# A list-scheduled transformer kernel: W2 loaded in two parts, task times corrected, and ranks for every step

## The chip, the cores and the metric

The kernel runs on one core of a Trainium2 chip. Time is device time in microseconds (us) of one execution, as the median of three runs; the profile is of one further execution of the same kernel. Engines are called by their names and by the short names of the profile: TensorE (PE, its weight loads PEld), VectorE (DVE), ScalarE (ACT), GpSimd (POOL) and SyncE (SP), whose queue issues the DMAs.

## The reference

Four layers over a sequence of 2048 rows of 512 in bfloat16: attention, MLP, attention, MLP, with the same weights both times. Attention is causal in a window of 256 rows, with 32 heads of 16.

```python
def _A_ref(x, wqkv, wo):
    B, S, D = x.shape
    H = 32; Dh = D // H; W = 256
    qkv = (x @ wqkv).reshape(B, S, 3, H, Dh).transpose(2, 0, 3, 1, 4)
    q, k, v = qkv[0], qkv[1], qkv[2]
    scores = jnp.einsum("bhqd,bhkd->bhqk", q, k) * (Dh ** -0.5)
    idx = jnp.arange(S)
    mask = (idx[:, None] - idx[None, :] >= 0) & (idx[:, None] - idx[None, :] < W)
    scores = jnp.where(mask[None, None], scores, -1e9)
    p = _softmax(scores, axis=-1)
    o = jnp.einsum("bhqk,bhkd->bhqd", p, v)
    return o.transpose(0, 2, 1, 3).reshape(B, S, D) @ wo

def _B_ref(x, w1, w2):          # w1: 512 x 1792, w2: 1792 x 512
    h = jnp.maximum(jnp.einsum("bsd,df->bsf", x, w1), 0)
    return jnp.einsum("bsf,fd->bsd", h, w2)

x = A_x
for layer in range(2):
    x = x + _A_ref(_layernorm(x), A_wqkv, A_wo)
    x = x + _B_ref(_layernorm(x), B_w1, B_w2)
```

## The kernel before

**Steps.** The sequence is cut into four chunks of 512 rows. A step is one chunk of one pair of layers (attention and MLP), so there are eight steps, k = 0 to 7; steps 4 to 7 are the second pair. In each step the chunk is normed and transposed (xnT), projected to Q, K and V (48 matmuls of 512 columns), attended, transposed again (OT), multiplied with wo, added to x, normed and transposed (xn2T), and sent through the MLP: 56 matmuls with W1 into hT and 56 with W2. Weights and x stay on the core.

**Attention.** K is spread into KBD and V into V2, ring buffers of 20 slots. Scores are made in groups into one PSUM tile of four banks (Sps); ScalarE takes the exponential of a group in one instruction of up to 2048 columns into Pb; GpSimd (with affine selects) or VectorE (with a minimum against the tile tri) sets masked entries to zero; TensorE multiplies with V2 into acc; VectorE divides. There are 156 score groups in all, 20 in a step and 16 in step 4. Their number along the sequence of groups is the "slot" in which most ranks of TensorE are counted.

**The planner.** The order of instructions is not written by hand. `plan_qkv`, `plan_attention` and `plan_rest` (lines 471, 541, 602) make tasks: `op(key, {engine: (us, function)}, deps, ...)` (line 229) with a rank `key`, the engines that can do the task with a time for each, and the tasks that it needs. Then a simulation of five engines walks through time. Whenever an engine is free, `choose` (line 734) takes one of its ready tasks: on TensorE that of lowest rank, on the others that of the lowest sum of ready time and rank. `begin` (line 755) emits its instructions at once. The result is one fixed order for each engine, and `InOrder` (line 104) chains each engine's instructions to keep it. On the chip, every engine works through its queue in that order and waits at semaphores; the planner's times play no part there any more.

A task with a third number, `(1.22, fn, 2.6)`, holds its engine for the first time and is complete after the second. SyncE's tasks have it: a transposing DMA of 128 rows (xnT, OT, xn2T) holds the queue for 1.22 us and lands 2.6 us after its start; the load of W2 (line 692) holds it for 1.4 us and lands after 9.0.

**Ranks on TensorE.** Scores have -100000 and their number, so they go first, in order. The multiplication with V2 has -50000 and more. wo has -10000 + k. Projections and MLP are filler with a rank in slots: those of a step `wait` = 16 slots ahead of its first score group (line 495), V at 1.6 slots from each other; those of the MLP spread from 7 to 24 slots after the end of the step's own scores (line 652), W1 over the first half and W2 over the second. Step 0 is worked in two halves (`HALVED`), with MLP parts from 8 to 18 slots after a given group (line 649). Dense matmuls share four PSUM buffers (`psum`, line 233).

**Other ranks.** `SOON` (line 194) has one rank for each kind of task, such as -1 for the copies to hT and for masks and -2 for additions to x. `calm` (line 477) holds back the norm statistics of steps 1, 2 and 3, by 1, 40 and 60. `act_free` (line 746) lets ScalarE take a task other than an exponential only if it ends at most 0.55 us after the next group can be exponentiated, or 0.1 us after a started group is done. If TensorE has had nothing for 0.4 us (line 802), the planner emits a filler matmul without use ("warm") against the slowing of the clock.

**Loads.** x and the weights come in at the start on SyncE's queue. W2 is a task of the planner: one DMA of 1.8 MB, free to go when the transposes of step 1's xnT (`applied[2]`) have landed.

Of the kernel before, what the change touches and what calls it, by code (L numbers as in the profile page):

```python
# [15 lines left out]
P = 128  # L16
# [22 lines left out]
]  # L39
PW = 576  # L40
SHOW = None

# [28 lines left out]
def kernel(  # L71
# [121 lines left out]

    SOON = {'qkv': -0.5, 'v': 0, 'h': -1, 'mask': -1, 'div': 0, 'add': -2}
    LINK = {"PE": 0.2, "DVE": 0.2, "ACT": 0.2, "POOL": 0.2, "SP": 0.2}

# [62 lines left out]

    EVAC = {512: {"DVE": 0.67, "ACT": 0.59}, 256: {"DVE": 0.42, "ACT": 0.38}}  # L260

# [20 lines left out]
    def norm_stats(lid, j, src, deps, eps_from=None, key=0):  # L282
        def fn():
            st = small.tile([P, 6], FP32, name="st", bufs=4)
            dve.bn_stats(out=st[:], in_=src)
            dve.bn_aggr(out=mvs[:, lid % 8, j, :], in_=st[:])
            if eps_from is not None:
                dve.tensor_scalar_add(rstds[:, lid % 8, eps_from:j + 1], mvs[:, lid % 8, eps_from:j + 1, 1], 1e-5)
        return op(key, {"DVE": (0.86 + (0.18 if eps_from is not None else 0), fn)}, deps)

    def norm_pow(lid, j0, j1, deps, key=0):
        r = rstds[:, lid % 8, j0:j1]
        return op(key, {"POOL": (0.72, lambda: pool.tensor_tensor(out=r, in0=r, in1=mhalf[:, j0:j1], op=ALU.pow))}, deps)

    def norm_apply(lid, j, src, deps, by_array, dst, then_key, dst_deps):

        box = Box(xns)
        mv, r, nb = mvs[:, lid % 8, j, :], rstds[:, lid % 8, j:j + 1], nbs[:, lid % 8, j:j + 1]

        def fn(e):  # L300
            box.t = box.tile([P, D], BF16, "xn")
            if e == "DVE":
                dve.tensor_scalar(out=box.t[:], in0=src, scalar1=mv[:, 0:1], scalar2=r, op0=ALU.subtract, op1=ALU.mult)
            else:
                pool.tensor_tensor(out=nb, in0=mv[:, 0:1], in1=r, op=ALU.mult)
                pool.tensor_scalar(out=nb, in0=nb, scalar1=-1.0, scalar2=None, op0=ALU.mult)
                pool.tensor_scalar(out=box.t[:], in0=src, scalar1=r, scalar2=nb, op0=ALU.mult, op1=ALU.add)
        times = {"DVE": 0.52} if by_array else {"POOL": 1.4, "DVE": 0.54}
        a = op(-10 if lid == 0 else 0, options(times, fn), list(deps) + list(dst_deps), box)
        if by_array:  # L310
            return transpose(then_key, lambda: box.t[:], lambda: dst[0][:, :, j * P:(j + 1) * P], [a], [box])

        def dma():
            sp.dma_start_transpose(out=dst[0][:, :, j * P:(j + 1) * P],
                                   in_=box.t[:].rearrange("p (kc d) -> p kc d", kc=KC))
        return op(0, {"SP": (1.22, dma, 2.6)}, [a], None, [box])

    def transpose(key, src, dst, deps, uses, take=None):
        box = Box(psum)

        def fn():
            box.ps = box.tile([P, KC, P], BF16, "tp")
            for kc in range(KC):
                pe.transpose(box.ps[:, kc, :], src()[:, kc * P:(kc + 1) * P], ident[:])
        t = op(key, {"PE": (0.26, fn)}, deps, box, list(uses) + [box])
        return op(0, options({"DVE": 0.42, "ACT": 0.59}, lambda e: copy(e, dst(), box.ps[:])), [t], take, [box])

# [119 lines left out]
    c_tri0 = op(-9, {"DVE": (0.2, lambda: dve.memset(tri[:], BIG))})  # L447
    c_tri = [op(3, {"POOL": (0.55, lambda i=i: triangle(i))}, [c_tri0]) for i in range(3)]
    c_v0 = [op(-6, {"POOL": (0.96, lambda s0=s0: pool.memset(V2f[:, 544 * s0:544 * (s0 + 4)].bitcast(FP32), 0.0))})
            for s0 in range(0, NSLOT, 4)]  # L450

    def v_ones(e):
        dve.memset(V2[64 * e:64 * e + 64, :, e, :, 16:17], 1.0)
    c_v = [op(-2, {"DVE": (0.4, lambda e=e: v_ones(e))}, c_v0) for e in range(2)]

# [15 lines left out]
    def plan_qkv(k):  # L471
# [4 lines left out]
        st, dst = [], []  # L476
        calm = (-10, 1, 40, 60)[k] if k < 4 else 0
        for j in range(4):
# [15 lines left out]
        old_pv = [pvs[n, j] for n in units_of.get(k - 2, []) for j in range(units[n].nq // 2)]  # L494
        wait = 0 if k == 0 else 16
        for h in range(2) if k == 0 else (None,):
# [5 lines left out]
            for t in range(4):  # L502
# [3 lines left out]
                def kmm(kc, ps, t=t, cols=cols):  # L506
                    mm(ps[:, cols], wqkv[:, kc, D + t * P:D + (t + 1) * P], xnT[0][:, kc, cols], kc == 0, kc == KC - 1)
                box, m = group(at, KC, us, kmm, need_x + [d_w[1]] + old[len(old) * t // 4:len(old) * (t + 1) // 4], lead=1000)
                times = {"DVE": 1.46, "ACT": 1.42} if h is None else {"DVE": 0.87, "ACT": 0.83}
                k_done[k, t, h or 0] = op(SOON["qkv"], options(times, lambda e, t=t, h0=h0, h1=h1, box=box:  # L510
                                                      spread_k(e, layer, c, t, h0, h1, box.ps)),
# [8 lines left out]
                def qev(e, t=t, cols=cols, box=box, idx=idx):  # L520
                    q = first(Q, (k, t), lambda: work.tile([P, 512], BF16, name="Qt", tag=f"Q{idx % 7}", bufs=1))
                    copy(e, q[:, cols], box.ps[:, cols])
                q_done[k, t, h or 0] = op(SOON["qkv"], options(EVAC[w], qev), [m2], None, [box])
                mine += [m, m2]
        for j in range(4):
            at = first_slot[units_of[k][0]] + (1 + (8 if j > 1 else 0) if k == 0 else 1.6 * j - wait)

            def vmm(kc, ps, j=j):
                mm(ps[:], xnT[0][:, kc, j * P:(j + 1) * P], wqkv[:, kc, 2 * D:3 * D], kc == 0, kc == KC - 1)
            box, m = group(at + 0.2, KC, 0.216, vmm, ([dst[j]] if k == 0 else dst) + [d_w[2]] + old_pv, lead=1000)  # L530
            vs = Box(stg)

            def vev(e, box=box, vs=vs):
                vs.t = vs.tile([P, 512], BF16, "Vst")
                copy(e, vs.t[:], box.ps[:])
            ev = op(SOON["qkv"], options(EVAC[512], vev), [m], vs, [box, vs])
            v_done[k, j] = op(SOON["v"], options({"POOL": 1.72, "DVE": 1.42} if k else {"POOL": 1.72, "DVE": 1.42, "ACT": 1.48}, lambda e, j=j, vs=vs: spread_v(e, layer, c, j, vs.t[:])),
                              [ev] + c_v, None, [vs])
            mine.append(m)

    def plan_attention(k):
        layer, c = divmod(k, NCH)
        prev = units_of.get(k - 1, []) if c else []
        for n in units_of[k]:
# [3 lines left out]
            for g in range(len(u.groups)):  # L548
# [17 lines left out]
                for m in u.masks(g):  # L566
                    times = {"DVE": 0.32 + 0.14 * (len(m) - 1), "POOL": 0.93 * len(m)}
                    masks[s].append(op(SOON["mask"], options(times, lambda e, m=m, g=g, pb=pb: mask(e, m, places(pb, g))), [exps[s]] + c_tri))
            for j0 in range(0, u.nq // 2, 2):
# [23 lines left out]
                def dfn(u=u, j=j, box=box):  # L593
# [3 lines left out]
                divs[k, u.t, j] = divs[k, u.t, j + 1] = op(  # L597
                    SOON["div"], {"DVE": (0.64, dfn)}, [prior] + war + checks[k - 2:k - 1], None, [box])
        checks.append(op(40, {"DVE": (1.1, lambda k=k: accumulate_check(chks[k % 2], k == 0))},
                         [divs[k, t, j] for t in range(4) for j in range(4)] + checks[-1:]))  # L600

    def plan_rest(k):
# [12 lines left out]
        for j in range(4):  # L615
# [8 lines left out]
            else:  # L624
                t = op(-5, {"SP": (1.22, lambda j=j, to=to: sp.dma_start_transpose(
                    out=to(), in_=O_of[k][:, j, :].rearrange("p (kc d) -> p kc d", kc=KC)), 2.6)}, ready, ob, [ob])
            turned[k, j] = t
# [4 lines left out]
            for o in [m]:  # L632
                o.uses.append(ob)
                ob.users += 1
            add = op(SOON["add"], {"DVE": (0.68, lambda j=j, box=box: residual(4 * c + j, box.ps[:], layer == 0))}, [m], None, [box])
            single = final and j >= 2
# [10 lines left out]
        for j0, j1 in ((0, 2), (2, 4)) if k in HALVED else ((0, 4),):  # L647
            if k in HALVED:
                d0 = first_slot[units_of[k][3 + 2 * j0]] + 8
                d1 = d0 + 10  # L650
            else:
                d0, d1 = base[k + 1] + 7, base[k + 1] + 24
            n0, n1 = P * j0, P * j1
            evs = []
            for f in range(NF):
# [6 lines left out]
                def hev(e, f=f, box=box, n0=n0, n1=n1):  # L662
                    if hT[0] is None:
                        hT[0] = work.tile([P, NF, 512], BF16, name="hT", tag="hT", bufs=1)
                    copy(e, hT[0][:, f, n0:n1], box.ps[:, n0:n1], True)
                evs.append(op(SOON["h"], options(EVAC[n1 - n0], hev), [m], None, [box]))
            for j in range(j0, j1):
                for n0, n1 in ((0, 256), (256, 512)) if final and j == 3 else ((0, 512),):
# [14 lines left out]
                    else:  # L683
                        x_done[k, j] = op(SOON["add"], {"DVE": (0.68, lambda j=j, box=box: residual(4 * c + j, box.ps[:], False))},
                                          [m, x_done[k, j], dst[j]], None, [box])

    plan_qkv(0)
    for k in range(NSTEP):
        plan_attention(k)
        if k == 0:  # L690
            plan_qkv(1)
            d_w2 = op(0, {"SP": (1.4, lambda: sp.dma_start(w2[:], B_w2.rearrange("(f p) n -> p f n", p=P)), 9.0)}, applied[2])
        plan_rest(k)
# [52 lines left out]
    def act_free(t, us):  # L746
# [4 lines left out]
        if scores[s].number in started:  # L751
            return t + us <= score_end[0] + 0.1
        return t + us <= max(t, scores[s].at("PE")) + 0.55

# [21 lines left out]
    while events and events[0][0] < 3000:  # L776
# [16 lines left out]
        for e in ENGINES:  # L793
# [7 lines left out]
            elif e == "PE" and done_ops[0] < len(ops) - 12:  # L801
                if t - idle_since[0] >= (0.4 if t > 20 else 0.0) and sum(1 for f, _ in psum.free if f <= t) > 1:
                    box = Box(psum)
# [166 lines left out]
```

## Time and profile before

| what | value |
|---|---|
| time, median of 3 | 482.74 us (481.2 to 483.36) |
| span of the profiled execution | 481.4 us |
| instructions | 14229 |
| exponentials on ScalarE | 282.6 us, 156 instructions |
| masks on GpSimd | 218.9 us, 498 instructions |
| transposing DMAs | 28 each of xnT, OT and xn2T, 2.5 us to landing |
| W1 and W2 | one DMA of 1792 KB each |

The page lists each engine's busy time and its share of the span, then the chain that ended last, followed backwards from the last instruction to what released it. Stage tables give, for a stretch of time, its length, the busy time of an engine with the number of its instructions, the clock that was granted to TensorE (1.00 is full), the share of time in which the DMA engines moved data, and GB/s. A timeline line has start, duration, engine, source line, operation, output and input, shape and count; in brackets stands the idle time before it and what ended it. Almost every instruction is recorded under line 114, the helper that all engines' calls go through, so one goes by the names of the tiles: ps_d is the output of a dense matmul, "w" stands for W1 and W2, Sps for scores, acc for the product with V.

### The profile page before, as it was taken

The page shows a single profiled execution, that of the slowest core. Times are in us where ns is not written, and L with a number is a line of the kernel's source. Part 1 is how long each engine was busy: PE and PEld are TensorE (multiplying, and loading weights), DVE is VectorE, ACT ScalarE, POOL GpSimd, SP SyncE. Part 2 cuts the span into 40 slices and gives each one's busy share as a digit, 9 for nine tenths or more (in the row PEclk, how much of TensorE's full clock was granted, in tenths as well). Part 3 has the DMA queues.
Part 4 walks back from the last instruction along what each step waited for, and adds up shares of the span by engine and source line. Part 5 has one row for each costly group of instructions (what it writes and reads, how often), then busy time and mean ns, then how long its engine had stood idle before and what let it go on. Part 6 is the DMA issues. An engine that isn't in the chain of part 4 may idle for free.

```text
span 481.4 us, 14229 instructions
## 1 busy us (share of the span) xinstructions
PE 457.3 (95%) x5893; PEld 244.7 (51%) x5967; DVE 354.4 (74%) x852; ACT 336.6 (70%) x263; POOL 299.5 (62%) x665
## 2 busy tenths in 40 slices
PE   8899999998999989999999999999999999999995
PEld 3555646654555534555554555544555545464443
DVE  6989988867986688977998878797558875464101
ACT  3878777876878657887778777777768777644230
POOL 7788878656786786856885766685766647421000
PEclk9999999999999989999999999999999999999998
DMA  8870321004300052002221023010331103000101
GB/s 247 276 200 3 67 23 25 2 3 67 59 9 3 8 84 45 3 3 45 57 35 33 15 23 67 11 38 2 45 78 25 34 1 68 25 1 11 34 12 38
DMA packets 54791, 21.96 MB, mean 46 GB/s; under 512 B 46144, under 2 KB 54208, under 8 KB 54720
## 3 DMA queue, kind: packets, MB, share of 16 engines
q1 hardware_dynamic: 54720, 20.98, 20.3%
q8 instruction: 48, 0.79, 0.7%
q14 instruction: 23, 0.19, 0.2%
HBM read 7.86 MB, written 2.10 MB: 21 GB/s over the span
## 4 chain that ended last, share of the span: by engine, by line
PE 77%; DVE 7%; POOL 5%; DMA 5%; issue 3%; ACT 1%; POOLq 0%; SPq 0%; DVEq 0%; ACTq 0%
PE ps_d L114 54%; PE acc L114 14%; PE Sps L114 8%; DMA OT<-O 3%; POOL Pb L114 3%; DVE KBD L114 2%; DVE st L114 1%; ACT Pb L114 1%; DVE x_sb L114 1%; POOL xn L114 1%; DMA xnT<-xn 1%; DVE Pb L114 1%; POOL rstds L114 1%; DMA x_sb<-in_A_x_dram 1%; DVE xn L114 1%
## 5 line engine op out<-in xcount | busy, mean ns | idle before, releaser
L114 ACT ACTIVATE Pb<-Sps 128x2048 bf16<-128x2048 f32 (+2 forms) x156 | 282.6, 1811 | 92.6 <-PE Sps L114 75.6
L114 POOL TENSOR_SCALAR_AFFINE_SELECT Pb<-Pb 64x256 bf16<-64x256 bf16 x498 | 218.9, 440 | 111.8 <-ACT Pb L114 91.6
L114 PE MATMUL ps_d<-xn2T,w 128*128 128x512 bf16 (+1 forms) x481 | 105.3, 355 | 2.5 <-issue 1.0
L114 PE MATMUL ps_d<-w,hT 128*128 128x512 bf16 (+1 forms) x438 | 103.8, 376 | 2.1 <-issue 1.3
L114 PEld LDWEIGHTS <-Pb 128*128 128x128 bf16 x2880 | 84.2, 96 | 26.6 <-issue 9.3
L114 PE MATMUL acc<-V2f,Pb 128*128 128x34 bf16 x2880 | 90.6, 178 | 2.6 <-POOL Pb L114 1.5
L114 DVE TENSOR_TENSOR Pb<-Pb,tri 128x512 bf16<-128x512 bf16 (+1 forms) x141 | 60.3, 433 | 16.5 <-ACT Pb L114 15.6
L114 PEld LDWEIGHTS <-w 128*128 128x128 bf16 x504 | 45.4, 97 | 44.6 <-issue 6.1
L114 PE MATMUL ps_d<-xnT,wqkv 128*128 128x512 bf16 (+1 forms) x277 | 64.9, 355 | 2.0 <-ACT KBD L114 0.9
L114 PEld LDWEIGHTS <-hT 128*128 128x128 bf16 x462 | 42.4, 98 | 46.6 <-issue 6.0
L114 PE MATMUL Sps<-Qt,KBD 32*128 32x320 bf16 (+3 forms) x1488 | 60.8, 251 | 1.3 <-ACT Pb L114 0.9
L114 DVE TENSOR_SCALAR hT<-ps_d 128x512 bf16<-128x512 f32 (+1 forms) x79 | 48.1, 619 | 16.3 <-PE ps_d L114 16.0
L114 PEld LDWEIGHTS <-KBD 32*128 32x128 bf16 x1488 | 23.4, 92 | 46.1 <-issue 42.9
L114 DVE TENSOR_SCALAR KBD<-ps_d,par 128x256 bf16<-128x256 f32 (+1 forms) x80 | 44.2, 601 | 1.4 <-PE ps_d L114 1.3
L114 DVE BATCH_NORM_STATS2 st<-x_sb 128x6 f32<-128x512 f32 (+1 forms) x64 | 43.7, 682 | 1.2 <-DMA x_sb<-in_A_x_dram 0.7
L114 DVE TENSOR_TENSOR x_sb<-ps_d,x_sb 128x512 f32<-128x512 f32 x48 | 32.4, 682 | 12.1 <-PE ps_d L114 11.4
L114 ACT ACTIVATE hT<-ps_d 128x512 bf16<-128x512 f32 (+1 forms) x47 | 26.2, 559 | 21.1 <-PE ps_d L114 21.1
L114 PEld LDWEIGHTS <-wqkv 128*128 128x128 bf16 x288 | 26.1, 97 | 25.6 <-issue 3.2
L114 PE MATMUL ps_d<-wo,OT 128*128 128x512 bf16 x121 | 32.6, 384 | 5.2 <-DMA OT<-O 4.4
L114 DVE TENSOR_TENSOR ob<-ps_d,x_sb 128x512 bf16<-128x512 f32 (+1 forms) x17 | 11.2, 659 | 34.4 <-PE ps_d L114 33.3
L114 POOL TENSOR_TENSOR rstds<-rstds,mhalf 128x2 f32<-128x2 f32 (+1 forms) x33 | 24.3, 738 | 16.7 <-DVE rstds L114 14.6
L114 PE MATMUL ps_d<-wqkv,xnT 128*128 128x512 bf16 x119 | 31.6, 379 | 0.3
(55 smaller groups left out, 279.9 us busy)
## 6 DMA issues: line engine op xcount, KB each, us to landing
w<-in_B_w_dram SPq DMA_DIRECT2D x2, 1792.0 KB, 10.6
out_dram<-ob SPq DMA_DIRECT2D x15, 128.0 KB, 1.7
wqkv<-in_A_wqkv_dram SPq DMA_DIRECT2D x3, 512.0 KB, 7.0
x_sb<-in_A_x_dram SPq DMA_DIRECT2D x3, 512.0 KB, 9.0
x_sb<-in_A_x_dram SPq DMA_DIRECT2D x2, 256.0 KB, 3.0
wo<-in_A_wo_dram SPq DMA_DIRECT2D x1, 512.0 KB, 8.8
xnT<-xn SPq DMA_TRANSPOSE x28, 2.5
OT<-O SPq DMA_TRANSPOSE x28, 2.5
```

Source lines behind the costliest of these rows:

```text
L114: inst = fn(*a, **k)
```

## The change

The planner stays, and so do all tasks of the computation. Three things change.

1. W2 is loaded by two DMAs of half the size, each planned as holding SyncE's queue for 3.6 us and landing after 5.0, the second after the first, with rank 3 in place of 0. In the plan no transposing DMA is issued during these 3.6 us. The aim is to keep the load and the transposes apart.
2. Times of tasks are corrected to those of a trace: VectorE's eviction of 512 columns 0.67 to 0.69, norm statistics 0.86 to 0.91, the power on GpSimd 0.72 to 0.75, the norm's application on GpSimd 1.4 to 1.58 and on VectorE 0.54 to 0.6, spreading V 1.72 to 1.85 on GpSimd and 1.42 to 1.35 on VectorE, masks, the division 0.64 to 0.72, the addition 0.68 to 0.69, and the landing of a transposing DMA 2.6 to 2.9.
3. Ranks that were one number for a kind of task are looked up in a table by kind and step, `tune(name, k, value)`, where `value` is the old number. The table has 98 entries: the ranks of SOON per step, of the norm's application, of the norm statistics ("calm"), the lead of the projections ("wait") and the pace of V, the start and length of the MLP ("from", "span"), ScalarE's allowance ("slack") and the idle time before a filler matmul ("idle", 0.4 to 0.81). The aim is an order with less waiting.

Two helpers that are added, `norm_stats_act` and `eps_op`, are called by nothing.

```diff
+TUNE = {
+    ("ones", 0): 3.74,
+    ("tri", 0): 2.04,
+    ("turn", 0): -0.63,
+    ("apply", 0): -14.88, ("apply", 1): -3.07, ("apply", 2): -3.19, ("apply", 3): -3.23, ("apply", 4): -1.45,
...
+    ("idle", 0): 0.81,
+    ("slack", 0): 0.91, ("slack", 1): 0.32,
+    ("qkv", 0): -3, ("qkv", 1): 0.71, ("qkv", 2): -0.94, ("qkv", 3): 0.47, ("qkv", 4): -2.62, ("qkv", 5): 1,
...
+    ("calm", 0): -6.45, ("calm", 1): 49.78, ("calm", 2): 55.35, ("calm", 3): 50.68,
+    ("wait", 1): 18.52, ("wait", 2): 20.9, ("wait", 3): 19.33, ("wait", 4): 15.48, ("wait", 5): 8, ("wait", 6): 9.3,
+    ("wait", 7): 18.77,
+    ("pace", 1): 0.2, ("pace", 2): 1.32, ("pace", 3): 1.71, ("pace", 4): 0.37, ("pace", 5): 1.05, ("pace", 6): 1.21,
+    ("pace", 7): 2.79,
+    ("from", 1): 6.7, ("from", 2): 5.71, ("from", 3): 4.61, ("from", 4): 11.02, ("from", 5): 9.1, ("from", 6): 3.64,
+    ("from", 7): 5.18, ("from", (0, 0)): 12.67, ("from", (0, 2)): 15.26,
+    ("span", 1): 29.93, ("span", 2): 16.39, ("span", 3): 33.16, ("span", 4): 36, ("span", 5): 16.73,
+    ("span", 6): 18.08, ("span", 7): 28.64, ("span", (0, 0)): 10.73, ("span", (0, 2)): 6.75,
+}
+def tune(name, k, value):
+    return TUNE.get((name, k), value)
...
+    def soon(name, k):
+        return tune(name, k, SOON[name])
...
-        return op(0, {"SP": (1.22, dma, 2.6)}, [a], None, [box])
+        return op(0, {"SP": (1.22, dma, 2.9)}, [a], None, [box])
...
-        calm = (-10, 1, 40, 60)[k] if k < 4 else 0
+        calm = tune("calm", k, (-10, 1, 40, 60)[k] if k < 4 else 0)
...
-        wait = 0 if k == 0 else 16
+        wait = 0 if k == 0 else tune("wait", k, 16)
...
-                d0 = first_slot[units_of[k][3 + 2 * j0]] + 8
-                d1 = d0 + 10
+                d0 = first_slot[units_of[k][3 + 2 * j0]] + tune("from", (k, j0), 8)
+                d1 = d0 + tune("span", (k, j0), 10)
             else:
-                d0, d1 = base[k + 1] + 7, base[k + 1] + 24
+                d0 = base[k + 1] + tune("from", k, 7)
+                d1 = d0 + tune("span", k, 17)
...
-            d_w2 = op(0, {"SP": (1.4, lambda: sp.dma_start(w2[:], B_w2.rearrange("(f p) n -> p f n", p=P)), 9.0)}, applied[2])
+            w2_in, d_w2 = B_w2.rearrange("(f p) n -> p f n", p=P), None
+            for f0, f1 in ((0, NF // 2), (NF // 2, NF)):
+                d_w2 = op(3, {"SP": (3.6, lambda f0=f0, f1=f1: sp.dma_start(w2[:, f0:f1, :], w2_in[:, f0:f1, :]), 5.0)},
+                          applied[2] + [d_w2])
...
-            return t + us <= score_end[0] + 0.1
-        return t + us <= max(t, scores[s].at("PE")) + 0.55
+            return t + us <= score_end[0] + tune("slack", 1, 0.1)
+        return t + us <= max(t, scores[s].at("PE")) + tune("slack", 0, 0.55)
...
-                if t - idle_since[0] >= (0.4 if t > 20 else 0.0) and sum(1 for f, _ in psum.free if f <= t) > 1:
+                if t - idle_since[0] >= (tune("idle", 0, 0.4) if t > 20 else 0.0) and sum(1 for f, _ in psum.free if f <= t) > 1:
```

## The prediction

> **What bounds the kernel now.** I read the page first: busy time by engine, then the chain that ended last.
>
> ```profile
> PE 457.3 (95%) x5893; PEld 244.7 (51%) x5967; DVE 354.4 (74%) x852; ACT 336.6 (70%) x263; POOL 299.5 (62%) x665
> ...
> PE 77%; DVE 7%; POOL 5%; DMA 5%; issue 3%; ACT 1%; POOLq 0%; SPq 0%; DVEq 0%; ACTq 0%
> ```
>
> TensorE is busy for 95% of the span and carries 77% of the chain; no other engine is above 74%. The change neither adds nor removes a matmul of the computation. So what it can win lies in two places only: TensorE's idle time, 481.4 - 457.3 = 24.1 us, and the filler matmuls ("warm") that the planner puts where it finds nothing ready. Next I cut the span into stages for TensorE (stage, busy time and count, granted clock, DMA share, GB/s):
>
> ```profile
> 10.00:30.00 20.00, 17.48 (x236) 1.00 0.80 251
> 30.00:50.00 20.00, 19.62 (x280) 1.00 0.28 78
> 50.00:70.00 20.00, 17.90 (x258) 1.00 0.33 50
> ...
> 100.00:122.00 22.00, 19.09 (x244) 1.00 0.30 46
> 122.00:170.00 48.00, 47.26 (x692) 1.00 0.10 19
> 170.00:182.00 12.00, 10.19 (x92) 0.86 0.44 69
> ...
> 280.00:420.00 140.00, 137.65 (x1851) 1.00 0.20 35
> ```
>
> The reader is to see that the holes are in the first 182 us. Idle time is 2.5, 2.1, 2.9 and 1.8 us in the stages 10-30, 50-70, 100-122 and 170-182; from 280 to 420 us it is 1.7% and made of pieces under 0.2 us where TensorE changes from one kind of work to another. The first 10 us (2.1 idle) are the first loads, the last 5.4 us are the last addition and store: neither is touched. The same stages for the filler give 2.1 us in 40-60, 3.4 us in 100-122, none after 140, and 7.4 us in the first 10. Then the timeline of TensorE in two holes:
>
> ```profile
> 113.00 0.81 PE L114 MATMUL warm<-ident 128*128 128x512 bf16 x3
> 114.02 0.40 PE L114 MATMUL Sps<-Qt,KBD 32*128 32x192 bf16 x8 [0.21 <-ACT Pb L114]
> 114.35 0.82 PE L114 MATMUL warm<-ident 128*128 128x512 bf16 x3
> ...
> 118.27 1.90 PE L114 MATMUL ps_d<-wo,OT 128*128 128x512 bf16 x8 [1.43 <-DMA OT<-O]
> ...
> 176.08 0.60 PE L114 MATMUL ps_d<-wo,OT 128*128 128x512 bf16 x2 [1.50 <-DMA OT<-O]
> ```
>
> These are two kinds of hole. Around 110-121 the planner itself saw nothing to do and filled: the projections of step 2 and the MLP of step 0 were used up, and the MLP of step 1 was not yet possible. At 116.8 and 174.6 the plan believed that OT would be there and it was not. The DMA issues say why: three or more transposes follow each other at 1.3 us, and then the later ones take longer. The first line is SyncE's timeline there, the second is over all 28 of OT.
>
> ```profile
> 112.75 4.95 SPq L114 DMA_TRANSPOSE OT<-O  x3
> ...
> DMA to landing us min/median/max: 2.4/2.5/4.2
> ```
>
> **What the Trainium skill says.** "TensorE: Matmul & The Clock Gate", part 2 (What happens when you issue a matmul): matmuls stay in program order, only weight loads are pulled ahead. The trace agrees: at 174.6 everything waited 1.50 us for one OT. So an order that is wrong at one place stops the whole engine. The same page, part 1: an idle window halves the clock. The row 170-182 shows 0.86, (1 - 0.86) x 12 = 1.7 us lost, after idle time of only 1.50 us; the equal hole at 116.8 cost no clock, so I count this half. "Perfetto Trace Analysis", Identifying the Most-Contended Engine, warns that matmul busy time overstates; the trace agrees (379 ns for a 512-column matmul that follows its neighbour after 0.22), so idle plus filler is a lower bound on the waste. "DMA: Bandwidth & Descriptors", Issuing engines are not separate DMA queues: all transfers share 16 engines and interleave. That bears on W2, next.
>
> **The change, part by part.**
>
> *W2 in two parts.* W2 is issued at 26.24 and takes
>
> ```profile
> DMA to landing us min/median/max: 8.1/8.1/8.1
> ```
>
> so it lands at 34.3; its first reader runs at 62.0. Two OT transposes are issued beside it at 32.77 and 34.02 and land 2.4 to 2.5 us later, the normal time, and in 30-40 TensorE is busy for 9.89 of 10 us: the sharing cost nothing visible. Half of W2 is 4.1 us (8.1/2) at best and, with the fixed part from the 256 KB load that took 3.0 us, 3.0 + 0.66 MB x (5.1 us / 1.57 MB) = 5.1 us at worst. Both parts end by 26.2 + 10.2, or some 10 us later if they give way to transposes; the 28 us of slack hide either. One more issue is 0.6 us of SyncE, which is idle. Behind it in SyncE's queue stand the OT transposes; in the plan each part holds that queue for 3.6 us. If both held up a transposition that TensorE needed, that would cost up to 7.2 us, against 0 if none. I take 0: at this place the transposes come 6.5 us after the last xnT issue.
>
> *Task times.* These only steer the plan. The new ones are nearer to the rows: the residual 0.69 (682 ns), hT on VectorE 0.69 (688 ns), statistics 0.91 (685 + 182 ns and a gap), division 0.72 (252 + 424 ns and a gap). Each correction is 0.01 to 0.18 us. The one that touches the holes is the transposition, 2.6 to 2.9; but the traces' late ones took 3.9 to 4.2. Of an error of 1.5 us, 0.3 is mended. So the waits for OT are not planned away; they go only where other work happens to stand in front.
>
> *Ranks.* These decide which ready task each engine takes. For TensorE the ones that count are the places of the projections ("wait" 16 becomes 8 to 21 score slots of lead) and of the MLP ("from", "span": 17 slots become 16 to 36). MLP(0) goes from 8 slots to 13 and 15: it is held back, and dense work is left for the hole at 110-121. A slot is 415/156 = 2.7 us, so 7 slots are 19 us. The wider spans (33 and 36 for steps 3 and 4) leave more for the pure dense tail after 428 us, which runs at 55.16 busy of 56, so nothing is lost there. For VectorE, "calm" of step 1 goes from 1 to 49.78, so its norm statistics run only when VectorE has nothing else; four times 0.87 us (685 + 182 ns), needed before the projections of step 1 at 29 us, are at risk. Steps 2 and 3 stood at 40 and 60 already. For ScalarE, "slack" rises from 0.55 to 0.91: an eviction may hold up an exponential by 0.36 us more. TensorE waits for exponentials for 0.9 us in all, so this is hidden while dense work is at hand.
>
> *The sum*, hole by hole. The share is my choice, by whether the planner can see the hole.
> - 10-30: 2.5 idle. The chain there is GpSimd (masks, V2, rstds); ranks reorder it but don't shorten it. A third: 0.8.
> - 40-70: 2.1 filler + 2.1 idle, of which 0.9 is a wait for OT. Half: 2.1.
> - 100-122: 3.4 filler + 2.9 idle, of which 2.0 is for OT. Mostly visible to the plan: 60% of 6.3 is 3.8.
> - 170-182: 1.8 idle + 1.7 clock, unplanned. Half: 1.7.
> - The other stages: 0, switching.
>
> Together 8.4. A new order in one in-order queue brings waits of its own kind; today's unplanned ones are worth 4.4 (all of TensorE's waits for OT), and I charge a quarter of these, 1.1. Net 7.3 to 7.4: 482.74 - 7.4 = 475.3.
>
> **The rivals.**
> *A, as above*, 475.3, in a band of 470 to 480.
> *B, all holes go*: 2.5 + 4.2 + 6.3 + 3.5 = 16.5 us, so 466.3. For it: there is dense work without end later (428 to 475 is nothing else), and 98 values are enough to place it. Against it: GpSimd binds in 10-30, and OT lateness isn't in the plan.
> *C, no change*: holes at 110-121 are filled, but transposes that come in threes and fours make as many new waits; 8.4 back and forth, 482. For it: the wait for OT is the longest named wait of TensorE (4.4 us, 4 times). Against it: filler is 5.4 us that the planner saw.
> *D, slower*: an order fitted to the plan to hundredths of a us breaks on the chip at another place, and one more hole like 100-122 (6.3) arises while only 2 are won: 482.7 + 6.3 - 2 = 487. For it: late statistics of step 1 ("calm" 49.8) and an MLP held too long (span 36 where a step has 20 slots, with one hT buffer, so that the next MLP waits for its last matmul). Against it: the planner knows these waits, and its TensorE costs (0.216 per matmul) are those of the trace.
>
> **How the numbers follow.** A 0.53, B 0.17, C 0.14, D 0.16. The range of 468 to 484 leaves out half of B and most of D, about 0.2. Within 0.5% means 480.3 to 485.2. Faster: A, B and a little of C, 0.73. Same: most of C with the edge of A, 0.11. Slower: D, 0.16.
>
> **What would show it.** If right: TensorE's busy time hardly falls except for the filler, its idle time falls from 24 to about 18; in the stage table the rows up to 122 us gain most; filler after 40 us shrinks from 20 matmuls to under 10; W2 shows two issues with no wait of TensorE near them, and its first reader doesn't wait for DMA. Waits for OT remain, 2 to 5 us. The last exponential may move, the dense tail gets longer or shorter by the same amount. Wrong: filler or idle time as before in 100-122 (C), a wait for statistics or xnT in 25-35 or for W2 near 62, a second stage with a clock under 1 (D), or a stage table without holes (B).

## The result, and the profile after

| what | before | after |
|---|---|---|
| time, median | 481.97 us (480.87 to 483.36) | 476.81 us (475.97 to 479.01) |
| ratio, 95% interval | | 0.9899 [0.9853, 0.9944] |
| span of the profiled execution | 481.4 us | 474.6 us |

The change makes the kernel faster by 5.2 us, 0.6 to 1.5%; 475.3 was predicted, within 468 to 484. (The forecast was a gain of 7.4 us, counted from the 482.74 that was then the median; the median of before in the table is 0.8 lower, so the time was met more closely than the gain.) The two profiled executions differ by 6.8 us, since the one of before (483.17 us) was above its median; its granted clock was 0.993, and most of before's executions have 0.996 or more. In what follows, one trace shows where time lies, and the medians how much it is.

The page of the changed kernel, busy time, chain and W2's issues (size of each, us to landing):

```profile
PE 451.7 (95%) x5890; PEld 242.8 (51%) x5963; DVE 348.1 (73%) x845; ACT 345.9 (73%) x277; POOL 299.4 (63%) x664
...
PE 82%; ACT 5%; DVE 5%; DMA 3%; issue 3%; POOL 2%; SPq 0%; ACTq 0%; DVEq 0%; POOLq 0%
...
w<-in_B_w_dram SPq DMA_DIRECT2D x2, 896.0 KB, 6.4
```

The share of TensorE in the chain rose from 77 to 82%: there is less of others to wait for. Its idle time is 474.6 - 451.7 = 22.9 us, hardly less than 24.1. Busy time fell by 5.6 us, though no matmul of the computation is gone. The filler is 1.8 us of that, and 1.7 us, as an estimate from the clock, is the stretch of half clock in before (177.6 to 181.0 us), in which matmuls take longer. The other 2.1 us aren't resolved; the recorded ends of matmuls may overlap differently when kinds of work alternate in another order. So idle time alone is not the measure here; the holes have to be counted by stage, with filler and clock. The stages of TensorE after (stage, busy time and count, clock, DMA share, GB/s):

```profile
10.00:30.00 20.00, 17.44 (x241) 1.00 0.58 192
30.00:50.00 20.00, 16.67 (x248) 1.00 0.60 133
50.00:70.00 20.00, 19.40 (x269) 1.00 0.14 28
...
100.00:122.00 22.00, 20.71 (x279) 1.00 0.30 50
122.00:170.00 48.00, 46.59 (x683) 1.00 0.18 32
170.00:182.00 12.00, 11.78 (x178) 1.00 0.15 30
```

The same stages for the filler matmuls alone:

```profile
10.00:30.00 20.00, 1.55 (x7) 1.00 0.58 192
30.00:50.00 20.00, 2.53 (x10) 1.00 0.60 133
...
100.00:122.00 22.00, 0.00 (x0) 1.00 0.30 50
```

and in before:

```profile
10.00:30.00 20.00, 0.27 (x1) 1.00 0.80 251
30.00:50.00 20.00, 2.05 (x8) 1.00 0.28 78
...
100.00:122.00 22.00, 3.36 (x12) 1.00 0.30 46
```

The reader adds, for each stage, idle time (length less busy time), filler, and what a clock under 1 takes:

| stage | before | after | change | predicted |
|---|---|---|---|---|
| 10-30 | 2.5 + 0.3 filler | 2.6 + 1.6 filler | +1.3 | -0.8 |
| 30-70 | 2.5 + 2.1 filler | 3.9 + 2.5 filler | +1.9 | -2.1 (for 40-70) |
| 100-122 | 2.9 + 3.4 filler | 1.3 | -5.0 | -3.8 |
| 122-170 | 0.7 | 1.4 | +0.7 | 0 |
| 170-182 | 1.8 + 1.7 clock | 0.2 | -3.3 | -1.7 |
| all others | | | -0.3 | 0 |
| new waits, no place named | | | | +1.1 |

They sum to -4.7 us of the 6.8 between the two spans; the other 2.1 are the unresolved busy time. The late holes went nearly whole; the early ones grew. The waits of TensorE (us in total, times, longest) name what is left, first in before, then in the changed kernel:

```profile
PE ps_d L114 <- DMA OT<-O: 4.4, 4, 1.5
...
PE Sps L114 <- ACT Pb L114: 0.9, 3, 0.5
...
PE tp L114 <- DVE xn L114: 0.5, 1, 0.5
```

```profile
PE Sps L150 <- ACT Pb L150: 3.0, 10, 0.6
PE tp L150 <- DVE xn L150: 2.2, 2, 2.0
...
PE ps_d L150 <- DMA OT<-O: 1.2, 2, 0.9
PE ps_d L150 <- DMA xnT<-xn: 1.2, 1, 1.2
```

Waits for OT fell from 4.4 to 1.2 us; waits for the exponential and for the first norm (xn, at 11.45 us) rose from 0.9 to 3.0 and from 0.5 to 2.2. The timeline of TensorE shows the place of step 1's projections and of wo in step 1:

```profile
40.94 0.81 PE L150 MATMUL ps_d<-xnT,wqkv 128*128 128x512 bf16 x3 [1.23 <-DMA xnT<-xn]
...
117.01 1.90 PE L150 MATMUL ps_d<-wo,OT 128*128 128x512 bf16 x8 [0.85 <-DMA OT<-O]
```

The projections of step 1 now begin at 40.9 us, since its statistics come late ("calm" 49.78). W2 follows them on SyncE's queue (start, time on the queue):

```profile
35.95 3.62 SPq L150 DMA_TRANSPOSE xnT<-xn  x2
39.62 1.18 SPq L150 DMA_DIRECT2D w<-in_B_w_dram  x2
```

The parts of W2 land at 45.0 and 47.6 us; TensorE first reads hT and W2 at 68.0. No wait of TensorE names W2.

### The profile page after: what moved, and what is told of

Read it like the earlier page. It is cut to its first block, busy times and chain, and to the rows that moved or that the text cites. A ratio compares the mean times of both kernels' runs of the same rounds, so it can differ in the third digit from the quotient of the medians.

```text
span 474.6 us, 14227 instructions
## 1 busy us (share of the span) xinstructions
PE 451.7 (95%) x5890; PEld 242.8 (51%) x5963; DVE 348.1 (73%) x845; ACT 345.9 (73%) x277; POOL 299.4 (63%) x664
## 4 chain that ended last, share of the span: by engine, by line
PE 82%; ACT 5%; DVE 5%; DMA 3%; issue 3%; POOL 2%; SPq 0%; ACTq 0%; DVEq 0%; POOLq 0%
PE ps_d L150 59%; PE acc L150 13%; PE Sps L150 9%; ACT Pb L150 4%; DMA OT<-O 2%; DVE V2f L150 1%; POOL Pb L150 1%; DMA xnT<-xn 1%; DMA x_sb<-in_A_x_dram 1%; PE tp L150 1%; DVE st L150 1%; DVE Pb L150 0%; DVE Vst L150 0%; POOL rstds L150 0%; DVE xn L150 0%
## 5 line engine op out<-in xcount | busy, mean ns | idle before, releaser
L150 POOL TENSOR_SCALAR_AFFINE_SELECT Pb<-Pb 64x256 bf16<-64x256 bf16 x504 | 221.8, 440 | 98.5 <-ACT Pb L150 72.2
L150 PEld LDWEIGHTS <-Pb 128*128 128x128 bf16 x2880 | 82.9, 96 | 21.3 <-issue 9.4
L150 PE MATMUL acc<-V2f,Pb 128*128 128x34 bf16 x2880 | 88.3, 178 | 0.7 <-POOL Pb L150 0.3
L150 DVE TENSOR_TENSOR Pb<-Pb,tri 128x256 bf16<-128x256 bf16 (+1 forms) x143 | 59.9, 429 | 16.9 <-ACT Pb L150 15.6
L150 PE MATMUL ps_d<-xnT,wqkv 128*128 128x512 bf16 (+1 forms) x275 | 63.3, 355 | 2.3 <-DMA xnT<-xn 1.2
L150 DVE TENSOR_SCALAR hT<-ps_d 128x512 bf16<-128x512 f32 (+1 forms) x66 | 39.6, 607 | 16.4 <-PE ps_d L150 15.7
L150 ACT ACTIVATE hT<-ps_d 128x512 bf16<-128x512 f32 (+1 forms) x60 | 33.9, 568 | 23.5 <-PE ps_d L150 22.2
L150 DVE TENSOR_SCALAR xn<-x_sb,mvs,rstds 128x512 bf16<-128x512 f32 (+1 forms) x45 | 25.0, 575 | 13.2 <-issue 9.3
L150 PE MATMUL ps_d<-wo,OT 128*128 128x512 bf16 x118 | 31.3, 380 | 1.9 <-DMA OT<-O 1.2
```

Of the source, the lines that this page charges most:

```text
L150: inst = fn(*a, **k)
```

## The experiments

Each comparison had its own runs of the kernel before, with medians of 481.97 to 482.3 us. The theory behind the first six: the gain is one of ranks, TensorE's above all, since W2 and the times bring no work forward. The rivals: the new times carry it; or only times and ranks together; or it is the luck of one order.

### One part alone

W2 in two parts, on the kernel before:

```diff
-            d_w2 = op(0, {"SP": (1.4, lambda: sp.dma_start(w2[:], ...), 9.0)}, applied[2])
+            for f0, f1 in ((0, NF // 2), (NF // 2, NF)):
+                d_w2 = op(3, {"SP": (3.6, ..., 5.0)}, applied[2] + [d_w2])
```

> The kernel before with W2 in two parts and nothing else. My theory: the load of W2 never ended a wait of TensorE, so 482 us, within 0.3% of before, and 30 to 40 us stays about 9.9 of 10 us busy. Rival (W2 collided with transposes): 1 to 2 us less, and the transposes of OT near 33 us land earlier after their issue than 2.4 us.

Measured: 482.70 us, ratio 1.0006 [0.9987, 1.0026]. The interval includes no change, as costed. TensorE's waits for OT stay:

```profile
PE ps_d L150 <- DMA OT<-O: 4.8, 6, 1.4
```

The times alone, with the old rank everywhere:

```diff
 def tune(name, k, value):
-    return TUNE.get((name, k), value)
+    return value
...
-        return op(0, {"SP": (1.22, dma, 2.6)}, [a], None, [box])
+        return op(0, {"SP": (1.22, dma, 2.9)}, [a], None, [box])
```

> The kernel before with the corrected task times only (old ranks, W2 in one part). My theory: the times only reshuffle the order, and the gain comes from ranks, so no gain: 482 with a scatter of 3 either way. Rival (true times are what gives a good order): 477 to 479, most of the gain.

Measured: 486.01 us, ratio 1.0074 [1.0046, 1.0103]: slower, by more than the scatter that either theory allowed. Times nearer to the chip's make a worse order when the ranks are those that went with the old times. TensorE's waits show three kinds that grew (before: 0.9, 0.5 and none listed):

```profile
PE Sps L150 <- ACT Pb L150: 4.1, 13, 0.6
PE tp L150 <- DVE xn L150: 3.1, 2, 2.0
PE ps_d L150 <- DMA xnT<-xn: 2.5, 3, 1.1
```

The ranks alone, on the old times:

```diff
+def tune(name, k, value):
+    return TUNE.get((name, k), value)
...
-        wait = 0 if k == 0 else 16
+        wait = 0 if k == 0 else tune("wait", k, 16)
```

> The kernel before with the 98 ranks only (old task times, W2 in one part). My theory: 477 to 479, most of the gain, with the filler of 110 to 121 us gone. Rival (ranks fit only with the times that they were chosen for): 481 to 484, with holes at other places than in the changed kernel.

Measured: 481.46 us, ratio 0.9976 [0.9964, 0.9989]: 0.6 us by the medians, 0.5 to 1.7 by the interval, far from the gain of the whole. The hole at 100-122 shrank here too (20.10 us busy of 22, no filler), but most of the wait for OT stayed and waits of other kinds grew (before: 4.4, 0.2 and 1.5):

```profile
PE ps_d L150 <- DMA OT<-O: 3.4, 7, 1.4
...
PE ps_d L150 <- DVE KBD L150: 2.2, 4, 1.0
PE acc L150 <- POOL Pb L150: 2.1, 2, 1.1
```

So the theory that ranks carry the gain by themselves falls, and so does the one that times do. Against the 482.06 us of before in these runs, W2 alone is +0.6, the times +4.0, the ranks -0.6, and all together are -5.2 in theirs: an interaction. The 98 ranks fit the times that they go with. Times and ranks together without W2 in two parts were not run, so whether the load has a part in it stays open.

### Which ranks

The changed kernel with the table used only for TensorE's dense work ("wait", "pace", "from", "span"), and its complement:

```diff
 def tune(name, k, value):
-    return TUNE.get((name, k), value)
+    return TUNE.get((name, k), value) if name in ("wait", "pace", "from", "span") else value
```

> The changed kernel with only those ranks left in the table that place TensorE's dense work (wait, pace, from, span); all other ranks are the old ones, new task times, W2 in two parts. Theory 1 (the dense work held back for 110 to 121 us is what gains): near 477 to 479, with no filler in 100 to 122. Theory 2 (each rank only fits with all others; after the times alone the order stood at 486.0): half way, 480 to 484.

> The complement: the changed kernel without wait, pace, from and span (old values), all other ranks new, new task times, W2 in two parts. Theory 1: the hole at 100 to 122 us comes back (some 5 us of idle time and filler) and the time is 482 or more. Theory 2: 482 to 485, holes somewhere in the first 180 us, not necessarily there.

Measured: TensorE's ranks alone 480.11 us, 0.9941 [0.9917, 0.9966]; the others alone 483.75 us, 1.0022 [1.0008, 1.0035]. Against the 486.0 of the times alone these are -5.9 and -2.3; both together give -9.2. (Both have W2 in two parts and the times alone don't; by the first experiment that is within 1.3 us.) On the right times they nearly add, and TensorE's make the larger part.

By its time, the first of the two is what the second theory said (480 to 484), though the hole at 100-122 is closed as in the first. The filler there in the complement:

```profile
100.00:122.00 22.00, 2.74 (x6) 0.92 0.17 22
```

With the old places of the dense work, the MLP of step 0 among it, filler (2.74 us), idle time (1.90) and a lower clock (0.92, 1.8 us) come back. With TensorE's ranks alone there is no filler there and 0.95 idle, but there is a hole further forward; its filler in 50-70:

```profile
50.00:70.00 20.00, 4.99 (x19) 1.00 0.30 55
```

The times alone, with all the old places, look much the same in these two stages:

```profile
50.00:70.00 20.00, 5.64 (x22) 1.00 0.36 55
...
100.00:122.00 22.00, 0.00 (x0) 1.00 0.21 20
```

So the later places aren't the only way to close the hole at 100-122, and closing it isn't by itself a gain: the times alone do it and are the slowest of all. What TensorE's ranks win over the times alone lies mostly behind it: idle time and filler fall from 4.3 to 2.6 us in 122-170 and from 4.2 to 1.8 in 182-280. The dense work is a stock: what fills one hole is missing in another.

### One rank: "calm" of step 1

The prediction named this one as a risk. Everything of the change kept, it is set back:

```diff
-    ("calm", 0): -6.45, ("calm", 1): 49.78, ("calm", 2): 55.35, ("calm", 3): 50.68,
+    ("calm", 0): -6.45, ("calm", 1): 1, ("calm", 2): 55.35, ("calm", 3): 50.68,
```

> The changed kernel with one rank set back: norm statistics of step 1 at 1 in place of 49.78. My theory, as in the prediction's risk: the late statistics make the changed kernel's new hole between 27 and 41 us (3.3 us idle and some 3.5 us filler), so this hole closes; if nothing opens instead, 472 to 474. Rival: early statistics only let the projections of step 1 run early, and the dense work that then is missing shows as a hole near 50 or 110 us: 477 to 481.

Measured: 483.86 us, ratio 1.0022 [1.0006, 1.0039]: the whole gain is gone, and neither theory reaches so far. The timeline of TensorE:

```profile
30.20 1.02 PE L150 MATMUL ps_d<-xnT,wqkv 128*128 128x512 bf16 x3 [1.95 <-DMA xnT<-xn]
...
52.03 0.29 PE L150 MATMUL Sps<-Qt,KBD 32*128 32x256 bf16 x4 [1.48 <-ACT Pb L150]
```

With early statistics the projections start at 30.2 us instead of 40.9. They fill 30-50 (19.63 busy of 20, where the changed kernel has 16.67), and then nothing is left at 52: 50-70 has 16.31 busy, 1.86 of it filler. So late statistics hold the projections back to where they are needed. This isn't the whole of the 7.1 us: in 10-70 the two traces differ by about 1.2 us only (idle time, filler and clock), and the rest lies in pieces up to 420 us, 122-170 the largest (idle and filler 4.5 against 1.4). The clock has a part: it was 0.985 to 0.995 in all 22 executions, 0.991 on average, and 0.994 to 0.999 in the changed kernel's four, 0.9965 on average; that is worth some 2.5 us, as an estimate from the two means. What is shown is that this one rank can't be taken out of the table; not that late statistics are good with other ranks.

### Luck of one order?

A task time is changed by 10 ns, which makes the planner emit another order. By the two traces, some 500 of TensorE's 5,890 matmuls change their place, all between 26 and 109 us; after that its order is the same:

```diff
-    EVAC = {512: {"DVE": 0.69, "ACT": 0.59}, 256: {"DVE": 0.42, "ACT": 0.38}}
+    EVAC = {512: {"DVE": 0.70, "ACT": 0.59}, 256: {"DVE": 0.42, "ACT": 0.38}}
```

> The changed kernel with one task time moved by 0.01 us (VectorE's eviction of 512 columns 0.70 in place of 0.69), which gives another order and changes nothing else. Theory A (the gain is a property of the ranks): within 1.5 us of the changed kernel, 475.5 to 478.5. Theory B (the gain is one lucky order among many that scatter by some 3 us, as the single edits so far did): anywhere from 476 to 484, more likely above 479.

Measured: 476.87 us, ratio 0.9891 [0.9862, 0.9919]. Another order of the early part, the same gain. So it doesn't hang on one listing of that part. How far other orders of the whole with these ranks would scatter isn't shown.

### Why OT comes late: instruction fetch

The prediction put late OT down to three or more transposes in a row. The traces say otherwise. In before, four follow each other at 1.3 us from 221.2 us, and each lands after 2.41 to 2.48. What stands beside the late ones is transfers of another kind, "instruction". Queue q8 has blocks of 16 KB: 48 in a run, one about every 10 us. The page counts 5890 matmuls and 5963 weight loads, and 11853 / 48 is 247, so it looks like one block in some 250 instructions of TensorE. Queue q14 has 23 blocks of 8 KB in a run; whose they are isn't shown. The fourteen profiled executions have 84 transposes each, 1176 in all: of 652 with no block of either queue in flight, none took over 2.8 us (median 2.45); of 524 with one, 328 did, up to 5.3. Both queues are needed for this: by q8 alone, 21 late ones would have nothing beside them.

That is a correlation. To move the blocks and leave the order alone, the fillers before 7 us are cut into four matmuls of 128 columns, some 96 instructions more (weight loads included) ahead of all else:

```diff
-                    d.opts = {"PE": (d.opts["PE"][0], lambda box=box: mm(
-                        box.tile([P, 512], FP32, "warm")[:], ident[:], ...
+                        n = 4 if t < 7 else 1
+                        for i in range(n):
+                            mm(w[:, 512 // n * i:512 // n * (i + 1)], ident[:], ...
```

> The changed kernel, same order of tasks, but each filler matmul before 7 us is cut into four of 128 columns, so that TensorE has 96 to 102 more instructions in its stream (in matmul and weight load) before its first useful one. In the traces so far a transposing DMA lands after 2.4 to 2.5 us, but after 3.3 to 4.6 us where a 16 KB fetch of instructions runs beside it[...]. Theory F (the fetch makes them late): the fetches come about 3.5 to 4 us earlier against the work, other transposes are late, those of OT near 112 to 115 us land in 2.5 us again, and the 1.0 us wait before wo near 116 us goes or shrinks; the total moves by 1 us or so, either way. Theory Q (lateness comes from transposes close behind each other, as the prediction said): the same transposes as in the changed kernel are late.

Measured: 479.10 us, ratio 0.9921 [0.9893, 0.995]. The queues of the DMA engines in the changed kernel from 113 to 115 us, beside OT (packets, MB, share of the time of the 16 engines in that window):

```profile
q8 instruction: 1, 0.02, 3.0%
```

and the time to landing of OT issued at 111-117 us, there and in the shifted kernel, where the block came at 111.4 us and none ran from 113 to 117:

```profile
DMA to landing us min/median/max: 3.3/4.0/4.6
```

```profile
DMA to landing us min/median/max: 2.5/2.5/3.0
```

The three of the changed kernel took 4.61, 3.95 and 3.34 us. In the shifted one the same three took 2.97 (the block still beside it), 2.50 and 2.48, so wo at 114.89 us starts without the wait of 0.85 us. The pair of xnT at 36 us went from 4.12 and 3.55 to 2.44 and 2.43 in the same way. But other blocks met other transposes. In the timeline of the shifted kernel, after OT of 257.6 and 258.9 us landed late (4.58 and 3.71 us, with blocks from 258.9 to 260.6):

```profile
262.23 0.39 PE L150 MATMUL ps_d<-wo,OT 128*128 128x512 bf16 x1 [1.75 <-DMA OT<-O]
```

All its waits for OT are 3.0 us. So the cause of lateness is shown by moving it; the time isn't better for it. The same shift on the kernel before, and a smaller one (fillers cut in two, some 32 instructions) on the changed kernel:

> The kernel before, same order of tasks, with the first fillers cut into four as in e8 (some 96 more instructions of TensorE at the start). Theory F (the fetch of instructions makes transposes late): the waits for OT near 63, 116 and 174 us (4.4 us in all) go or shrink and others come; the total moves by 1 to 3 us, 479 to 484. If it falls to 479 or less, over half of the change's gain was the luck of where fetches fell; if it stays at 481 or more, the order itself carries the gain. Theory Q: same late transposes, 482.

> The changed kernel, same order, with the first fillers cut in two (some 32 more instructions of TensorE at the start), so that fetches come about 1.2 us earlier than in the changed kernel. Theory F: another set of late transposes again, with the total within 475 to 480; the pair of xnT near 36 and 37 us, late in the changed kernel at a distance of 0 to 1.3 us from a fetch, is late only if the fetch still starts inside its flight.

Measured: before shifted 482.88 us, 1.0013 [0.9994, 1.0033], its waits for OT 5.2 us; after with the small shift 477.60 us, 0.9897 [0.9862, 0.9931]. After's three positions are 476.8, 477.6 and 479.1, a mean of 477.8; before's two are 482.0 and 482.9, a mean of 482.4. So some 4.6 us, as an estimate, belong to the order. What the place of the blocks is worth isn't resolved: after's three lie 2.3 us apart by their medians and 1.2 by their ratios, and their intervals overlap. The clock takes part in it. In the trace of the first shift, half clock follows the wait at 262 us (263.8 to 267.2), and the four of its six executions with a clock of 0.994 or 0.995 took 479.1 to 479.8 us, the two others 477.2 and 477.3.

### A time that was still wrong, and new ranks

In the changed kernel TensorE waits 2.02 us at 11.45 for the first norm. The timeline of VectorE shows what stood ahead of it:

```profile
10.62 0.33 DVE L150 MEMSET V2f<- 64x320 bf16 x1 [1.14 <-issue]
10.98 0.74 DVE L150 TENSOR_SCALAR xn<-x_sb,mvs,rstds 128x512 bf16<-128x512 bf16 x2
```

The second of two memsets of V2's ones is shown; the first, at 9.16 us, is the same with 1.05. Each is planned at 0.4 us, and with the time in front of it holds VectorE for 1.4; what that time is, the profile doesn't show. The planner is told so; in the second kernel, all 98 ranks are also fitted anew to these times:

```diff
-    c_v = [op(tune("ones", 0, -2), {"DVE": (0.4, lambda e=e: v_ones(e))}, c_v0) for e in range(2)]
+    c_v = [op(tune("ones", 0, -2), {"DVE": (1.45, lambda e=e: v_ones(e))}, c_v0) for e in range(2)]
...
-    ("idle", 0): 0.81,
+    ('idle', 0): 1.65,
...
-    ("calm", 0): -6.45, ("calm", 1): 49.78, ...
+    ('calm', 1): 36.11,
```

> The changed kernel with one task time mended that the correction had left out: setting the ones of V2 on VectorE, planned at 0.4 us, takes 1.4 to 1.5 in the traces with its wait (0.33 busy after 1.05 to 1.14), so 1.45. In the changed kernel two of these stand in front of two norm applications and TensorE waits 2.0 us at 11.45. Theory (the wait is real loss): it goes, 474.5 to 476. Rival (the order reshuffles and TensorE runs out of work later, as with calm): 476 to 478.5, the hole moves to 27 to 41 us.

> The kernel of e11 (V2's ones at 1.45) with all 98 ranks fitted anew to this plan. Theory A (a better fit to truer times pays on the chip): 473 to 475.5. Theory B (what the plan doesn't know, where the fetches fall, is now as large as what is left): 475.5 to 479, no better than the changed kernel.

Measured: 476.02 us, 0.9859 [0.9828, 0.9889]; and 475.25 us, 0.9841 [0.9808, 0.9874]. The second has the lowest median of all, but the intervals of both overlap that of the changed kernel. With the time corrected the wait for the norm went, and another stood behind it; TensorE's waits:

```profile
PE ps_d L150 <- DMA wqkv<-in_A_wqkv_dram: 1.5, 1, 1.5
...
PE tp L150 <- DVE xn L150: 0.3, 1, 0.3
```

The sign of the rival came as well: 30-50 has 3.72 us of filler where the changed kernel has 2.53, and a clock of 0.83. With new ranks, there is no filler in 30-50 (the rank "idle" asks for 1.65 us of nothing first), and the clock is lower still. Its stage:

```profile
30.00:50.00 20.00, 17.00 (x249) 0.74 0.59 133
```

Up to (1 - 0.74) x 20 = 5.2 us are lost there, as estimated from the clock alone. Whether the time feels it isn't shown: with the corrected time and the old ranks, the executions at a clock of 0.990 and 0.992 took 475.3 and 476.8 us, those at 0.996 475.4 to 476.2. Filler with these ranks was not tried.

## Why the prediction was right or wrong

**The bound.** Right: matmuls that wait for order, none that are saved. But idle time was to fall to 18 us and fell to 22.9. The sum idle + filler + clock by stage was the better measure. (Three small readings are off: the 55.16 us busy of 56 are those of 420 to 476, not of the time after 428; TensorE's last matmul ends 5.9 us before the end, not 5.4; and the transposes of OT come 6.5 us after the issue of W2, 7.8 after that of the last xnT. None enters the sum.)

**W2 at nothing.** Right: 1.0006 alone. The slack seen as 28 us turned out as 20 (47.6 to 68.0), and the parts came later than assumed, after the late transposes of xnT.

**Times "only steer".** Right in kind; that they steer to a worse order with the old ranks (+4 us) was not seen. A correction of 0.01 to 0.18 us each looked too small to matter, but the planner chooses at each step, and 10 ns move some 500 matmuls.

**Ranks of TensorE.** Right in part: with the new times, the other new ranks and the old places the hole at 110-121 comes back, but the times alone, also with the old places, have no filler there. The hole at 100-122 gave 5.0 us instead of 3.8, and 170-182 gave 3.3 instead of 1.7: 8.3 where 5.5 were booked. Of these, 1.7 is the clock, which belongs to the trace of before and to a minority of its executions (see below).

**The step that failed: the shares of the early holes.** For 10-30 and 40-70 the prediction booked -0.8 and -2.1; measured are +1.3 and +1.9 (30-70). Their sign is wrong, 6.1 us in all. Filler after 40 us did fall, from 20 matmuls to none, but 15 of them (4.08 us) now stand in 27-36, where before had none: the hole moved. It goes with the late statistics of step 1, which hold its projections back to 40.9 us and which the prediction named as a risk and put at nothing in its sum. The two kernels with the old "calm" (TensorE's ranks alone, and the one rank set back) have no filler from 10 to 50 us; the complement, with the new "calm" and TensorE's old ranks, has 3.31 us in 30-50. With the new waits at +0.7 (1.1 booked) the ledger closes at -4.7 and the medians at -5.2, where -7.4 was forecast. That it came near is partly luck: an error of 2.8 in the late holes covered nearly half of that in the early ones.

**"Calm" of step 1.** Wrong sign. Named as a risk for A and as evidence for D, it is a rank without which the gain is gone (483.86).

**Late OT.** Wrong cause: not transposes in a row, but a fetch of instructions beside them. The conclusion drawn from it, that a planned landing of 2.9 us can't plan the waits away, holds for this cause as well. Predicted 2 to 5 us of waits for OT; the changed kernel has 1.2, and 3.0 with the fetches shifted, so the 1.2 is partly luck.

**The clock.** "The Trainium skill", page "TensorE: Matmul & The Clock Gate", part 1, speaks of windows of about 3.4 us and has half clock follow an idle window. The traces agree with the length: every stretch at half clock that ends before its kernel does lasts a multiple of 3.41 us (177.6 to 181.0 in before). They don't agree with the condition. Cut into pieces of 3.41 us in step with these changes, the fourteen traces have 16 pieces at full clock that half clock follows, and TensorE was busy for 39 to 63% of each of them (56% in before, from 174.2 us). No piece that was busier was followed by it; between 42 and 63% both occur, and what decides there isn't shown. So a gap of 1.5 us can cost the clock, and not in every execution: of 56 executions of the kernel before, ten had a mean clock of 0.995 or less and a median of 484.1 us, the other 46 one of 481.9. The trace of before is of the smaller kind. To count half of the 1.7 us was therefore not too careful: all of it went between the two traces, but the medians hold little of it.

**The rivals.** D listed a wait for xnT in 25-35 as its sign. It came at 40.9, with 1.23 us, and D did not: one wait is no verdict on an order. B is out (early holes stay), C is out by the interval.

## What to carry to other kernels

Ranks of a list scheduler and the times that they were fitted with are one thing: correct the times and the ranks have to be fitted again, or the order gets worse. Count a hole as idle time plus filler plus lost clock, stage by stage, and ask of each hole that a change fills where the work was taken from. A wait seen in one trace may be a matter of where the instruction fetches fall, so shift them (a few instructions more at the start) before it is explained by the order. And set traces side by side only with their granted clocks: a stretch of half clock can come in one execution of a kernel and not in the next.

## What the runs showed of the hardware

A transposing DMA (128 rows of 512 in bf16 within the core's memory) lands after 2.45 us (median) if no block of instructions is fetched meanwhile (652 of 652 under 2.8), also as the fourth in a row; with a fetch beside it, 328 of 524 took 2.8 to 5.3 us. "The Trainium skill", page "Runtime: NRT & Kernel Launch", Instruction fetch mechanics, has such blocks of 16 KB for 256 instructions, which fits the 48 of 16 KB here, and calls the cost "mostly hidden". For matmuls no run here shows anything against that; for a transpose that the next matmul waits for, it isn't hidden. How the fetch holds up the transpose isn't shown by any run.

Beside a plain load, transposes were not late: of 37 that ran next to a load of W2, the eight with no fetch in flight landed after 2.4 to 2.5 us.
